# Strassen's method in the second block's first product, and a reordered first block

## The chip, the cores and the metric

The kernel runs on one core of a Trainium2 chip. The time is that of the device, in microseconds (us), from one execution to the next of the same program; the profile is that of one further execution. Engines go by their short names: PE is TensorE's matmul, PEld its weight load, DVE VectorE, ACT ScalarE, POOL GpSimd, SP SyncE, which only issues DMAs here.

## The reference

```
attn_out = decay attention of q, k, v, f        # batch 4, 8 heads, 576 tokens, head width 64
x = attn_out as 2304 tokens x 512
h = x @ w_in                                    # 512 x 2048, first block
g = where(h >= 1, h, where(h <= -1, 0, (h + 1) ** 2 / 4))
x = g @ w_out                                   # 2048 x 512
h = x @ w_in2                                   # second block, same sizes
g = (a0 + a1 h + a2 h^2 + a3 h^3) / (1 + |b0||h| + |b1|h^2 + 1e-6)
out = g @ w_out2
```

All of it is float32. The weights come as 64-bit numbers and are turned into float32 on the chip.

## The kernel before

Every product of float32 matrices is made of three fast matmuls: each operand is split into a high part (`xh`, `wh`, `gh`) and the rest (`xl`, `wl`, `gl`), and high by low, low by high and high by high are added up in PSUM. The split takes one cast on ACT and one subtraction on DVE or POOL.

The program has three stages. The first is attention over 16 pairs of heads, with some work of the first block (`filling`) laid between: the weight conversions of `w_steps`, and for two chunks of tokens the first four slices of the hidden width. The second stage is the first block, the third the second block. Both blocks go through the 2304 tokens in five chunks (`CH` = 512, 512, 512, 512, 256) and through the 2048 hidden units in 16 slices `g` of 128. For a chunk `x` and a slice `g`, `gemm_in` (L758) makes a tile h of 128 hidden units by the chunk's tokens with 4 x 3 matmuls, the activation turns it into g, `split_g_hi` and `split_g_lo` split it, and `gemm_out` adds its share to the chunk's accumulators (L852 in the first block, L854 in the second). The tiles h have four PSUM banks (tag `h`), the accumulators the other four (`a0` to `a3`), and there are three pairs of buffers for gh and gl.

The first block's activation is `a11` (clip of h to -1..1, DVE L777), `a12` (square, ACT L782) and `a21` (maximum with h, DVE L786). The second block's is a chain over ACT (`b_abs` L793, `b_sq` L796, `b_lin` L799, `b_ln` L814, `b_exp` L817), DVE (L807, L811, L821, L824, L828) and POOL (L803), and ends with `b_t4`, which frees the PSUM bank.

A planner (`plan`) sets the order of all this: each `task` has a key, an engine, an expected duration, the tasks it depends on, and the buffers it takes and frees. The planner lays the tasks out one after the other by the time at which each could start, plus a small weight times the key. The table `NUDGE` moves the keys of numbered tasks. The result is a fixed order of instructions on each engine, and an engine executes its own in that order. SP issues all DMAs, in its own fixed order.

## Time and profile before

| | |
|---|---|
| time, median of 3 runs | 971.06 us (970.61 to 971.22) |
| the profiled execution's own time | 970.89 us |
| its span, first to last instruction | 969.2 us |
| PE busy | 956.1 us, 99% of the span |
| DVE, ACT, POOL busy | 73%, 65%, 45% |
| mean granted clock of TensorE | 0.997 of full speed |

Busy time is an average over stages: attention takes the first 215 us or so, the first block runs from there to about 570 us, the second block to the end.

### The profile page before, as it was taken

What the parts mean: (1) busy time and instruction counts of PE and PEld (TensorE: products, weight loads), DVE (VectorE), ACT (ScalarE), POOL (GpSimd) and SP (SyncE); (2) the same over time, 40 slices, a digit from 0 to 9 for tenths busy, and PEclk for the clock granted to TensorE, in tenths of its full rate; (3) what the DMA queues carried; (4) which work ended last, traced back from release to release, by engine and by line L of the source; (5) the groups of instructions that cost most, each with busy time, mean ns of one, the idle gap of its engine ahead of it and who ended that gap; (6) DMA issues with size and microseconds to landing.
All of it is one profiled execution on the core that took longest, in us unless ns stands there. A gap on an engine that the chain in (4) does not pass through costs nothing.

```text
span 969.2 us, 15465 instructions
## 1 busy us (share of the span) xinstructions
PE 956.1 (99%) x5124; PEld 783.1 (81%) x5124; DVE 707.6 (73%) x1391; ACT 629.7 (65%) x1327; POOL 436.0 (45%) x490
## 2 busy tenths in 40 slices
PE   8999999999999999999999999999999999999998
PEld 5667777778888888888888998888888888888887
DVE  7898889963878967867755779776666766766565
ACT  6999888875654434334334579777677677766675
POOL 3766745636455422322221235444445454444444
PEclk9999999999999999999999999999999999999999
DMA  7897798756553565755742650010101100010010
GB/s 231 256 287 236 230 284 283 246 174 197 189 192 110 163 209 161 238 174 158 244 131 88 196 168 7 1 44 0 44 12 33 44 1 23 0 44 1 1 44 23
DMA packets 66656, 125.14 MB, mean 129 GB/s; under 512 B 10048, under 2 KB 20944, under 8 KB 66576
## 3 DMA queue, kind: packets, MB, share of 16 engines
q1 hardware_dynamic: 66576, 124.16, 40.0%
q8 instruction: 40, 0.66, 0.3%
q14 instruction: 40, 0.33, 0.1%
HBM read 94.61 MB, written 29.51 MB: 128 GB/s over the span
## 4 chain that ended last, share of the span: by engine, by line
PE 80%; DVE 2%; ACT 1%; issue 0%; POOL 0%; ACTq 0%
PE h L758 38%; PE a L854 20%; PE a L852 17%; PE T L533 1%; PE O L570 1%; PE a L839 1%; PE S L469 1%; DVE wd L113 1%; DVE wd L107 0%; DVE wd L101 0%; PE S L460 0%; ACT wh L127 0%; ACT t L782 0%; DVE t L786 0%; POOL wl L131 0%
## 5 line engine op out<-in xcount | busy, mean ns | idle before, releaser
L772 POOL TENSOR_TENSOR gl<-t,gh 128x512 fp32r<-128x512 f32 (+1 forms) x160 | 196.3, 1228 | 278.7 <-ACT gh L768 202.2
L758 PE MATMUL h<-xh,wl 128*128 128x512 f32 (+1 forms) x640 | 236.9, 370 | 0.2 <-POOL wl L131 0.2
L758 PE MATMUL h<-xl,wh 128*128 128x512 f32 (+1 forms) x640 | 235.5, 368 | 0.0
L758 PE MATMUL h<-xh,wh 128*128 128x512 f32 (+1 forms) x640 | 235.5, 368 | 0.0
L768 ACT CAST gh<-t 128x512 fp32r<-128x512 f32 (+1 forms) x160 | 93.0, 582 | 117.1 <-PE a L854 47.2
L803 POOL TENSOR_TENSOR t<-t,t 128x512 f32<-128x512 f32 (+1 forms) x80 | 94.5, 1181 | 129.5 <-ACT t L796 121.2
L758 PEld LDWEIGHTS h<-xh,wl 128*128 128x128 f32 x640 | 120.6, 188 | 20.9 <-POOL wl L131 0.6
L758 PEld LDWEIGHTS h<-xh,wh 128*128 128x128 f32 x640 | 120.6, 188 | 20.0
L758 PEld LDWEIGHTS h<-xl,wh 128*128 128x128 f32 x640 | 120.7, 189 | 19.8
L854 PE MATMUL a<-wh,gl 128*128 128x512 f32 x288 | 112.2, 389 | 0.0
L854 PE MATMUL a<-wl,gh 128*128 128x512 f32 x288 | 112.2, 389 | 0.0
L854 PE MATMUL a<-wh,gh 128*128 128x512 f32 x288 | 112.0, 389 | 0.0
L852 PE MATMUL a<-gh,wl 128*128 128x512 f32 (+1 forms) x288 | 105.3, 366 | 0.0
L852 PE MATMUL a<-gl,wh 128*128 128x512 f32 (+1 forms) x288 | 105.3, 365 | 0.0
L852 PE MATMUL a<-gh,wh 128*128 128x512 f32 (+1 forms) x288 | 105.2, 365 | 0.0
L782 ACT ACTIVATE t<-t 128x512 f32<-128x512 f32 (+1 forms) x80 | 47.1, 589 | 75.8 <-DVE t L777 75.6
L777 DVE TENSOR_SCALAR t<-h 128x512 f32<-128x512 f32 (+1 forms) x80 | 50.8, 635 | 60.2 <-PE h L758 59.7
L821 DVE SCALAR_TENSOR_TENSOR t<-t,na,h 128x512 f32<-128x512 f32 (+1 forms) x80 | 55.3, 691 | 53.3 <-ACT h L817 52.4
L521 ACT ACTIVATE P<-P,nm 128x384 f32<-128x384 f32 (+3 forms) x144 | 84.1, 586 | 15.6 <-DVE nm L509 14.6
L807 DVE TENSOR_TENSOR t<-h,t 128x512 f32<-128x512 f32 (+1 forms) x80 | 51.0, 637 | 55.4 <-ACT t L799 55.1
L238 POOL TENSOR_SCALAR_AFFINE_SELECT cb<-cb 128x128 f32<-128x128 f32 (+1 forms) x150 | 56.2, 387 | 62.9 <-DVE nm L509 47.4
L793 ACT ACTIVATE t<-h,ab 128x512 f32<-128x512 f32 (+1 forms) x80 | 51.8, 649 | 43.5 <-PE h L758 43.5
(121 smaller groups left out, 1883.6 us busy)
## 6 DMA issues: line engine op xcount, KB each, us to landing
raw<-in_moe_w_in_dram SPq DMA_DIRECT2D x32, 512.0 KB, 3.7
raw<-in_moe_w_out_dram SPq DMA_DIRECT2D x32, 512.0 KB, 4.2
xr<-xd SPq DMA_DIRECT2D x48, 256.0 KB, 3.9
wfd<-wd SPq DMA_DIRECT2D x42, 256.0 KB, 4.2
wf<-wfd SPq DMA_DIRECT2D x42, 256.0 KB, 2.6
cb<-cd SPq DMA_DIRECT2D x15, 576.0 KB, 9.4
ks<-in_k_dram SPq DMA_DIRECT2D x16, 288.0 KB, 4.7
qs<-in_q_dram SPq DMA_DIRECT2D x16, 288.0 KB, 4.7
```

The lines of the kernel that those rows point to most:

```text
L238: POOL.affine_select(out=t, in_=t, compare_op=ALU.is_ge, fill=-BIG, base=0, pattern=[[-1, n]], channel_multiplier=1,)
L521: ACT.activation(p, p, AF.Exp, scale=-1.0, bias=nm[pr][:, pos:pos + 1], accum_out=ls[pr][:, COL[pos]:COL[pos] + 1])
L758: PE.matmul(hps[g], ww[:, kk * P:(kk + 1) * P], xx[kk], start=(kk == 0 and y == 0), stop=(kk == KD - 1 and y == 2))
L768: ACT.copy(gt[g][0], mid[g][0])
L772: eng.tensor_tensor(out=lo, in0=mid.pop(g)[0], in1=hi.bitcast(F32), op=ALU.subtract)
L777: DVE.tensor_scalar(out=c, in0=hps[g], scalar1=-1.0, scalar2=1.0, op0=ALU.max, op1=ALU.min)
L793: ACT.activation(mid[g]["w"], hps[g], AF.Abs, scale=ab[:, 0:1])
L803: POOL.tensor_tensor(out=vv, in0=vv, in1=mid[g]["w"], op=ALU.add)
L807: DVE.tensor_tensor(out=t, in0=hps[g], in1=t, op=ALU.mult)
L821: DVE.scalar_tensor_tensor(out=t, in0=t, scalar=na[:, 0:1], in1=hps[g], op0=ALU.add, op1=ALU.mult)
L852: PE.matmul(acc[x, d], ww[:, dd], gg, start=st, stop=sp)
L854: PE.matmul(acc[x, d], gg[:, dd], ww[:], start=st, stop=sp)
```

## The change

In the second block, the first product is taken for six parts of 384 tokens, two at a time (three groups `s`), and for pairs of slices, g = 2j and 2j+1 (eight values of `j`). For each of the 24 steps (s, j), the pair of slices and the pair of token parts by the two halves of the 512-long sum form a product of 2 x 2 blocks. Strassen's method, in Winograd's form, makes it of seven products of blocks (`q_mul`, numbered 1, 2, 7, 6, 4, 5, 3 in the order in which they run) where eight were needed; each is 2 x 3 matmuls of 384 columns. Products 1, 6 and 5 and then 3 add up in one PSUM bank (written h<s>_<j>_0 below), 7 and 4 in a second (_1), 2 in a third (_2); a fourth (_3) takes a sum. Between them `q_copy` copies a bank to SBUF after products 1, 7 and 6 (below c1, c7 and c6; on ACT or DVE), and `q_add` on DVE adds such a copy to a bank after products 2, 4 and 5 (below a2, a1 and a3). Product 6 has to wait for c1, 4 for c7, 5 for c6, and 3 for a3, since each of them writes on in the bank that is read there. The four sums are the four tiles h of the step, and each goes through the second block's activation as before, on 384 columns.

The sums of weight blocks (`q_sums`, on DVE or POOL) are made once during the first block, split, and stored in DRAM; `q_load` brings a step's four operands back, for each group s anew, into a ring of six slots. The sums of token parts (`p_sum`) are made for each group and stored too, and `u_load`, `u_hi` and `u_lo` load and split the operands of a group. The second product (`gemm_out2`) is as before, for parts of 384 tokens: three accumulators (`a0` to `a2`), so that the fourth bank is free for the sums.

In the first block, `a11` becomes a relu on ACT, `a12` squares it, and `a21` takes max(h, 1) and the minimum of the two in one DVE instruction. The chunk of 256 tokens now comes before the last pass of a 512 chunk. In attention, the scores of query block 0 are made together with those of block 1, and pair 0's first inputs are brought in by two DMAs (`ct`) instead of four. `NUDGE` is a new table.

```diff
     def load_c(pr):
...
+        if not pr:
+            for x in range(2):
+                SP.dma_start(ct[0][x:P:QB, :].bitcast(F32), ft[0:2, 2 + x, :].bitcast(F32))
+            return
...
-            for x in range(2):
-                SP.dma_start(ct[0][j * QB + x:j * QB + x + 1, :].bitcast(F32), ft[j:j + 1, 2 + x, :].bitcast(F32))
...
-                qc = slice(b * P, (b + 1) * P)
+                parts = [(b, slice(0, (b + 1) * P))] + [(0, slice(2 * P, 3 * P))] * (b == 1)
                 for x, (qq, kk_) in enumerate(((ql_, kh), (qh, kl_), (qh, kh)) + (((one, c_),) if pr == 0 else ())):
+                    for bb_, to in parts:
+                        for jj in range(2):
+                            pp = slice(jj * QB, (jj + 1) * QB)
+                            PE.matmul(
+                                ts[jj][:, to], qq[pp, bb_ * P:(bb_ + 1) * P] if x < 3 else qq[pp, :],
+                                kk_[pp, 0:(bb_ + 1) * P], start=(x == 0 and bb_ == b),
+                                stop=(x == (2 if pr else 3)), skip_group_check=(b == 1),
+                            )
...
     def a11(g, n):
-        c = t_new(g, "t0", n, 2 if filling else TN[0])
         s = t_new(g, "t1", n, SF if filling else TN[1])
-        DVE.tensor_scalar(out=c, in0=hps[g], scalar1=-1.0, scalar2=1.0, op0=ALU.max, op1=ALU.min)
-        mid[g] = [s, c]
+        ACT.activation(s[:, 0:n], hps[g], AF.Relu, scale=0.5, bias=0.5)
+        mid[g] = [s]
 
     def a12(g):
-        s, c = mid[g]
-        ACT.activation(s, c, AF.Square, scale=0.5, bias=0.5)
+        s = mid[g][0][:, 0:hps[g].shape[1]]
+        ACT.activation(s, s, AF.Square)
 
     def a21(g):
-        s = mid[g][0]
-        DVE.tensor_tensor(out=s, in0=hps.pop(g), in1=s, op=ALU.max)
+        h = hps.pop(g)
+        s = mid[g][0][:, 0:h.shape[1]]
+        DVE.scalar_tensor_tensor(out=s, in0=h, scalar=1.0, in1=s, op0=ALU.max, op1=ALU.min)
...
+    def q_sums(j, i, e):
+        wg, wo = (wst[1, 2 * j + k, 0] for k in range(2))
+        a = [w[:, (2 * c + i) * P:(2 * c + i + 1) * P] for w in (wg, wo) for c in range(2)]
+        t = wsum[j, i] = t_new(f"q{j}", "t0", DM, TN[0])
+        s1, s2, s3, s4 = (t[:, k * P:(k + 1) * P] for k in range(4))
+        eng = ENGINES[e]
+        eng.tensor_tensor(out=s1, in0=a[2], in1=a[3], op=ALU.add)
+        eng.tensor_tensor(out=s2, in0=s1, in1=a[0], op=ALU.subtract)
+        eng.tensor_tensor(out=s3, in0=a[0], in1=a[2], op=ALU.subtract)
+        eng.tensor_tensor(out=s4, in0=a[1], in1=s2, op=ALU.subtract)
+
+    def q_hi(j, k):
+        src = wst[1, 2 * j + k, 0] if k < 2 else wsum.pop((j, k - 2))
+        hi = homes.pop(0).bitcast(F32R)
+        wq[j, k] = (hi, src)
+        ACT.copy(hi, src)
+
+    def q_lo(j, k, e):
+        hi, src = wq[j, k]
+        lo = (homes.pop(0) if k < 2 else src).bitcast(F32R)
+        wq[j, k] = (hi, lo)
+        ENGINES[e].tensor_tensor(out=lo, in0=src, in1=hi.bitcast(F32), op=ALU.subtract)
+
+    def q_store(j, k):
+        hi, lo = wq.pop((j, k))
+        c = slice(HQ * P * (k == 1), DM)
+        SP.dma_start(wqd[j, k, 0][:, c], hi[:, c].bitcast(F32))
+        SP.dma_start(wqd[j, k, 1][:, c], lo[:, c].bitcast(F32))
+        homes.extend([hi.bitcast(F32)] + [lo.bitcast(F32)] * (k < 2))
+
+    def q_load(s, j, k, c0):
+        r = ring.pop(0)
+        t = slot(r) if r >= W_EARLY else wearly.tile([P, 2, DM], F32R, tag=f"w0_{r}", name=f"q{s}_{j}_{k}")
+        wring[s, j, k] = r, t
+        SP.dma_start(t[:, :, c0:].bitcast(F32), wqd[j, k, :, :, c0:].rearrange("y p n -> p y n"))
...
+    def p_sum(s, i, y, e):
+        o, a, b = (xq[s, i, c][:, 0:QN] for c in TSUMS[y])
+        ENGINES[e].tensor_tensor(out=o, in0=a, in1=b, op=ALU.subtract)
...
+    PRODUCTS = {
+        1: (0, 0, "a", 0, True), 2: (0, HQ, "b", 2, True), 7: (None, 2, "f", 1, True), 6: (None, 1, "e", 0, False),
+        5: (None, 0, "d", 0, False), 4: (1, HQ, "g", 1, False), 3: (None, 3, "c", 0, False),
+    }
+    bank = {}
+
+    def h_new(s, j, n, spare):
+        if n == 2 and not spare:
+            t = psA.tile([P, 512], F32, tag="a3", name=f"h{s}_{j}_{n}")
+        else:
+            t = psH.tile([P, 512], F32, tag="h", name=f"h{s}_{j}_{n}")
+        bank[s, j, n] = t[:, 0:QN]
+
+    def q_mul(s, j, n, spare):
+        part, c0, y, bk, new = PRODUCTS[n]
+        if new:
+            h_new(s, j, bk, spare)
+        o = bank[s, j, bk]
+        for i in range(HQ):
+            if part is None:
+                w, c = wring[s, j, 2 + i][1], c0 * P
+            else:
+                w, c = wring[s, j, part][1], (c0 + i) * P
+            wh, wl = (w[:, z, c:c + P] for z in range(2))
+            xh, xl = xu[y, i]
+            for z, (ww, xx) in enumerate(((wl, xh), (wh, xl), (wh, xh))):
+                PE.matmul(
+                    o, ww, xx, start=(new and i == 0 and z == 0), stop=(i == HQ - 1 and z == 2), skip_group_check=True,
+                )
+        if n == 3:
+            hps[2 * j, 2 * s] = o
+        for k in {2: (0,), 4: (1,), 3: (2, 3)}.get(n, ()):
+            ring.append(wring[s, j, k][0])
+
+    def q_add(s, j, n):
+
+        to, add, v = {1: (2, 2, (2 * j, 2 * s + 1)), 7: (3, 0, (2 * j + 1, 2 * s)), 6: (1, 1, (2 * j + 1, 2 * s + 1))}[n]
+        if to == 3:
+            h_new(s, j, 3, False)
+        hps[v] = bank[s, j, to]
+        DVE.tensor_tensor(out=hps[v], in0=bank[s, j, add], in1=us.pop((s, j, n)), op=ALU.add)
+
+    def q_copy(s, j, n, e):
+        us[s, j, n] = xp.tile([P, NM], F32, tag="xr", name=f"us{s}_{j}_{n}", bufs=XR)[:, 0:QN]
+        copy(e, us[s, j, n], bank[s, j, PRODUCTS[n][3]])
+
+    def gemm_out2(x, g, d):
+        if g == 0:
+            acc[x, d] = psA.tile([P, 512], F32, tag=f"a{d}", name=f"b{x}_{d}")
+        (gh, gl), (wh, wl) = gt[g, x], wt[1, g, 1]
+        dd = slice(d * P, (d + 1) * P)
+        for y, (gg, ww) in enumerate(((gl, wh), (gh, wl), (gh, wh))):
+            PE.matmul(acc[x, d], gg[:, dd], ww, start=(g == 0 and y == 0), stop=(g == NF - 1 and y == 2))
...
-    passes = [(0, x, early) for x in range(FILL, HEAD)] + [(0, x, late) for x in range(HEAD)]
-    passes += [(0, x, range(NF)) for x in range(HEAD, NCH)]
-    passes += [(1, x, range(NF)) for x in range(NCH, 2 * NCH)]
+    passes = [(0, x, early) for x in range(FILL, HEAD)] + [(0, x, late) for x in range(HEAD - 1)]
+    passes += [(0, x, range(NF)) for x in range(HEAD, NCH)] + [(0, HEAD - 1, late)]
...
+            t = task(key, "act", ca, lambda g=g: a12(g), (t,))
+            t = task(key, "dve", cd + 0.06, lambda g=g: a21(g), (t,), (), ("h",))
...
+            prev_in = p1 = mul(1, [ql[0]], ("h",))
+            c1 = cpy(1, p1)
+            prev_in = p2 = mul(2, [], (cbank,), ("r",))
+            a2 = addu(1, (p2, c1))
+            prev_in = p7 = mul(7, [ql[2], ql[3]], ("h",))
+            c7 = cpy(7, p7)
+            prev_in = p6 = mul(6, [c1])
+            c6 = cpy(6, p6)
+            prev_in = p4 = mul(4, [c7, ql[1]], (), ("r",))
+            a1 = addu(6, (p4, c6))
+            prev_in = p5 = mul(5, [c6])
+            a3 = addu(7, (p5, c7), ("h",))
+            prev_in = p3 = mul(3, [a3], (), ("r", "r"))
+            now = []
+            for g, x, t, hb in ((2 * j, 2 * s + 1, a2, cbank), (2 * j + 1, 2 * s, a3, "h"), (2 * j, 2 * s, p3, "h"), (2 * j + 1, 2 * s + 1, a1, "h")):
+                v = (g, x)
+                ta = task(key, "act", cs + 0.09, lambda v=v: b_abs(v, QN), [t, *last_t], ("t0", "t1", "t2"))
...
+    for n, x in enumerate(2 * s + 1 - c for s in range(NSUP) for c in range(2)):
+        for g in range(NF):
+            key = K2 - LEAD + LAG + (n * NF + g) * step / 4
+            t = gsplit = task(key - KS2, "act", ca, lambda v=(g, x): split_g_hi(v, QN), (tg[g, x], gsplit), ("g",))
+            t = task(key - KS2, "pool", cp, lambda v=(g, x): split_g_lo(v, POOL), (t,), (), ("t1",))
+            for d in range(QN // P):
+                tout = last_out[d] = task(
+                    key, "pe", mm(DM, 3), lambda x=x, g=g, d=d: gemm_out2(x, g, d),
+                    [t, wd[1, g, 1], last_out.get(d), tout], (f"a{d}",) if g == 0 else (), ("g",) if d == QN // P - 1 else ()
...
-        (648, 29, -0.8), (1339, 23, 1.6), (1564, 5, 0.5), (1173, 66, -1.2), (4043, 36, 0.6), (240, 8, -16.0),
...
+        (1307, 58, 1.3), (1243, 58, 6.2), (792, 35, -3.0), (618, 16, -8.4), (1400, 59, 0.8), (884, 3, 5.1),
```

PE, in the second block of the kernel before, at chunk 7 (512 tokens) and slice 5: h7_5 is the tile (its last three matmuls), a6_0 an accumulator of the chunk before.

```order
L758 MATMUL h7_5_8901<-xh7_3_8635,wl0_1_5_6709 128x512
L758 MATMUL h7_5_8901<-xl7_3_8639,wh0_1_5_6708 128x512
L758 MATMUL h7_5_8901<-xh7_3_8635,wh0_1_5_6708 128x512
L854 MATMUL a6_0_8286<-wh1_1_14_7360,gl_8829 128x512
L854 MATMUL a6_0_8286<-wl1_1_14_7361,gh_8828 128x512
L854 MATMUL a6_0_8286<-wh1_1_14_7360,gh_8828 128x512
```

PE, in the changed kernel, at step s = 2, j = 3, from the end of product 4 to product 3 and past it: b2_0 to b2_2 are the accumulators of the second product, u and q (or arena) the operands.

```order
L1029 MATMUL h2_3_1_10429<-ul3_9754,q2_3_1_10305 128x384
L1029 MATMUL h2_3_1_10429<-uh3_9753,q2_3_1_10305 128x384
L1029 MATMUL h2_3_0_10384<-arena_3838,q2_3_2_10181 128x384 x3
L1029 MATMUL h2_3_0_10384<-arena_3838 128x384 x3
L1055 MATMUL b2_0_9984<-w1_1_12_7596,gl_10392 128x512
L1055 MATMUL b2_0_9984<-w1_1_12_7596,gh_10391 128x512 x2
L1055 MATMUL b2_1_9994<-w1_1_12_7596,gl_10392 128x512
L1055 MATMUL b2_1_9994<-w1_1_12_7596,gh_10391 128x512 x2
L1029 MATMUL h2_3_0_10384<-arena_3838,q2_3_2_10181 128x384 x3
L1029 MATMUL h2_3_0_10384<-arena_3838 128x384 x3
L1055 MATMUL b2_2_10003<-w1_1_12_7596,gl_10392 128x512
L1055 MATMUL b2_2_10003<-w1_1_12_7596,gh_10391 128x512 x2
```

The tile's twelve matmuls in a row have become products of six. Between product 5 (h2_3_0, after h2_3_1) and product 3 (h2_3_0 again), between which a3 stands, there are six matmuls of the second product; between products 4 and 5 there is nothing.

ACT, in the second block of the kernel before, at the same tile h7_5.

```order
L793 ACTIVATE t0_5_8926<-h7_5_8901,ab_68 128x512
L796 ACTIVATE t2_5_8928<-h7_5_8901,rt_69 128x512
L799 ACTIVATE t1_5_8927<-h7_5_8901,na_67 128x512
L768 CAST gh_8957<-t1_1_8750 128x512
L814 ACTIVATE t0_5_8926<-t2_5_8928 128x512
L817 ACTIVATE h7_5_8901<-t0_5_8926 128x512
L793 ACTIVATE t0_6_8969<-h7_6_8944,ab_68 128x512
```

ACT, in the changed kernel, from the end of step s = 0, j = 6 into j = 7: us0_7_7 is the copy c7, us0_7_6 the copy c6, L843 the logarithm, L846 the exponential that writes back to the bank, L793 here the cast to gh, L822, L825 and L828 the three that were L793, L796 and L799, L996 the cast of a token operand.

```order
L793 CAST gh_8295<-home_6796 128x384
L822 ACTIVATE t0_14_1_8300<-h0_7_2_8270,ab_68 128x384
L843 ACTIVATE t0_12_0_8240<-t2_12_0_8241 128x384
L825 ACTIVATE t2_14_1_8301<-h0_7_2_8270,rt_69 128x384
L397 COPY us0_7_7_8324<-h0_7_1_8303 128x384
L828 ACTIVATE t1_3840<-h0_7_2_8270,na_67 128x384
L397 COPY us0_7_6_8339<-h0_7_0_8231 128x384
L843 ACTIVATE t0_14_1_8300<-t2_14_1_8301 128x384
L846 ACTIVATE h0_6_0_8067<-t0_12_0_8240 128x384
L996 CAST arena_3838<-arena_3838 128x384
L846 ACTIVATE h0_7_2_8270<-t0_14_1_8300 128x384
```

Operations of one tile stood together; now those of two tiles of a step and of the next step are mixed, and the copies c7 and c6 of step 7 stand ahead of the exponential of step 6's tile h0_6_0, that of product 3.

## Rows read from the trace of the kernel before

**Rows 1.** The page's part 1: busy time, share of the span, instructions.
```profile
span 969.2 us, 15465 instructions
PE 956.1 (99%) x5124; PEld 783.1 (81%) x5124; DVE 707.6 (73%) x1391; ACT 629.7 (65%) x1327; POOL 436.0 (45%) x490
```

**Rows 2.** Busy time by stretch: PE, PEld, DVE, ACT, POOL; PEclk, DMA share, GB/s.
```profile
12.00:100.00 88.00, 83.05 (x637) 59.87 (x635) 78.29 (x250) 80.68 (x241) 55.05 (x98) 0.98 0.83 260
100.00:215.00 115.00, 113.32 (x881) 86.79 (x877) 99.17 (x300) 100.01 (x284) 63.06 (x113) 1.00 0.78 249
215.00:570.00 355.00, 354.79 (x1736) 300.68 (x1733) 253.28 (x400) 158.93 (x283) 124.34 (x97) 1.00 0.54 175
570.00:905.00 335.00, 335.00 (x1505) 278.43 (x1504) 235.53 (x348) 245.17 (x413) 161.53 (x126) 1.00 0.08 24
905.00:945.00 40.00, 40.00 (x228) 35.15 (x227) 20.82 (x50) 25.10 (x63) 17.35 (x21) 1.00 0.08 27
966.00:969.20 3.20, 0.00 (x0) 0.00 (x0) 0.22 (x1) 0.00 (x0) 0.00 (x0) 0.73 0.44 164
```

**Rows 3.** Chain that ended last: start, length, what, matmuls in it.
```profile
588.65 2.72 PE a L854 x12
591.37 2.72 PE h L758 x12
...
901.45 4.31 PE h L758 x36
```

**Rows 4.** Timeline of PE in attention: pairs of 384-column matmuls on half arrays.
```profile
123.17 0.35 PE L469 MATMUL S<-kl,qh 64*128 64x384 f32 x2
123.34 0.35 PE L469 MATMUL S<-kh,qh 64*128 64x384 f32 x2
```

**Rows 5.** Groups by shape, PE, whole span: count; busy, mean ns; idle before.
```profile
L758 PE MATMUL h<-xh,wl 128*128 128x512 f32 x512 | 200.7, 392 | 0.2 <-POOL wl L131 0.2
...
L758 PE MATMUL h<-xh,wl 128*128 128x256 f32 x128 | 36.1, 282 | 0.0
```

**Rows 6.** Timeline in the second block: a tile's last matmul, ACT, then DVE.
```profile
653.54 0.39 PE L758 MATMUL h<-xh,wh 128*128 128x512 f32 x1
...
653.97 0.69 ACT L793 ACTIVATE t<-h,ab 128x512 f32<-128x512 f32 x1 [0.31 <-PE h L758]
...
655.12 0.78 ACT L799 ACTIVATE t<-h,na 128x512 f32<-128x512 f32 x1
...
655.94 0.69 DVE L807 TENSOR_TENSOR t<-h,t 128x512 f32<-128x512 f32 x1 [0.17 <-ACT t L799]
```

**Rows 7.** Groups by shape, DVE and ACT, 570 to 960 us.
```profile
L807 DVE TENSOR_TENSOR t<-h,t 128x512 f32<-128x512 f32 x64 | 44.2, 691 | 41.4 <-ACT t L799 41.2
L807 DVE TENSOR_TENSOR t<-h,t 128x256 f32<-128x256 f32 x16 | 6.8, 422 | 14.0 <-ACT t L799 13.9
L793 ACT ACTIVATE t<-h,ab 128x512 f32<-128x512 f32 x64 | 44.3, 693 | 43.5 <-PE h L758 43.5
L793 ACT ACTIVATE t<-h,ab 128x256 f32<-128x256 f32 x16 | 7.5, 475 | 0.0
L381 ACT COPY osb<-a 128x512 f32<-128x512 f32 x8 | 4.7, 592 | 1.2 <-PE a L854 1.2
L381 ACT COPY t<-a 128x256 f32<-128x256 f32 x4 | 1.4, 388 | 0.0
```

**Rows 8.** Groups by shape, DVE and ACT, 20 to 215 us.
```profile
L777 DVE TENSOR_SCALAR t<-h 128x512 f32<-128x512 f32 x8 | 5.5, 689 | 1.7 <-PE h L758 1.6
...
L782 ACT ACTIVATE t<-t 128x512 f32<-128x512 f32 x8 | 5.1, 633 | 3.7 <-DVE t L777 3.7
```

**Rows 9.** PE's waits, whole span: total us, times, longest.
```profile
PE S L460 <- DMA ct<-ft: 1.0, 1, 1.0
```

**Rows 10.** Timeline of SP at the start: the four DMAs of ct.
```profile
7.00 2.48 SPq L233 DMA_DIRECT2D ct<-ft  x4
```

**Rows 11.** The page's part 6: DMA issues, KB each, median us to landing.
```profile
raw<-in_moe_w_in_dram SPq DMA_DIRECT2D x32, 512.0 KB, 3.7
```

More of the change, by code (lines that the diff above doesn't have):

```diff
@@ L123, in s0 @@
         def s0():
-            pool = wearly if g < W_EARLY else wpool["late"]
             at["s"] = wst.pop((m, g, half))
-            at["w"] = [pool.tile([P, DM], F32R, tag=f"{x}{half}_{g}", name=f"w{x}{half}_{m}_{g}") for x in "hl"]
-            ACT.copy(at["w"][0][:], at["s"])
+            if half == 0 and g >= W_EARLY:
+                t = slot(g)
+            else:
+                pool = wearly if g < W_EARLY else wpool["late"]
+                t = pool.tile([P, 2, DM], F32R, tag=f"w{half}_{g}", name=f"w{half}_{m}_{g}")
+            at["w"] = [t[:, 0, :], t[:, 1, :]]
+            ACT.copy(at["w"][0], at["s"])
         def s1(eng=POOL):
             hi, lo = at["w"]
-            eng.tensor_tensor(out=lo[:], in0=at["s"], in1=hi[:].bitcast(F32), op=ALU.subtract)
+            eng.tensor_tensor(out=lo, in0=at["s"], in1=hi.bitcast(F32), op=ALU.subtract)
             wt[m, g, half] = (hi, lo)
@@ L749 @@
     hps, gt, mid, acc, po = {}, {}, {}, {}, {}
+    given = {}
     def gemm_in(m, x, g, kks):
@@ L761, in gemm_in @@
                 )
+        if kks[-1] == KD - 1 and not filling:
+            ring.extend(given.get((x, g), ()))
+    homes = []
     def t_new(g, tag, n, bufs):
+        if tag == "t1" and not filling:
+            return homes.pop(0)
         return tp.tile([P, NM], F32, tag=tag, name=f"{tag}_{g}", bufs=bufs)[:, 0:n]
@@ L1036, with more_small @@
     last_out = {}
-    prev_in = None
+    prev_in = gsplit = None
+    a11s, ins = [], {}
+    PREP = ((4, 10), (4, 15)), ((3, 7), (3, 10)), ()
+    LA = (XSLOT - W_EARLY) * 2 * DM
+    GIVES = {g: ([g] if g < XSLOT else [], []) for g in range(NF)}
+    for g in range(XSLOT):
+        GIVES[g][1].append("r")
+    for n, (y, i) in enumerate(UNITS):
+        GIVES[W_EARLY + (LA + (n + 1) * 2 * QN - 1) // (2 * DM)][1].append(f"u{y}{i}")
+    NSM = 4 * DM // QN
+    def more_small():
+        t = wpool["late"].tile([P, 4 * DM], F32, tag="tail", name="tailh")
+        homes.extend(t[:, k * QN:(k + 1) * QN] for k in range(NSM))
     for p, (m, x, fs) in enumerate(passes):
@@ L1085 @@
-            t = task(key, "act", ca, lambda g=g, n=n: split_g_hi(g, n), (t,), ("g",))
-            t = task(key, "pool", cp, lambda g=g: split_g_lo(g, POOL), (t,), (), ("t1",))
-            for d in range(nd):
+                deps = [prev_in, wd[0, g, 0]] + [sx[kk] for kk in kks if one]
+                prev_in = task(key, "pe", mm(n, 3 * len(kks)), lambda x=x, g=g, kks=kks: gemm_in(0, x, g, kks), deps,
+                               ("h",) if kks[0] == 0 else (),
+                               (tuple(f"x{kk}" for kk in kks) if end else ()) + (tuple(gone) if kks[-1] == KD - 1 else ()))
@@ new lines @@
+            t = tin = ins[x, g] = prev_in
+            lastg = ends and end
+            t = task(
+                key, "act", cs + 0.09, lambda g=g, n=n, lastg=lastg: (a11(g, n), lastg and more_small()), (t, *a11s[-1:], *(qstored.values() if lastg else ())),
+                ("t1",), ("t1",) * NSM if lastg else ()
+            )
+            a11s.append(t)
+            t = task(key, "act", ca, lambda g=g: a12(g), (t,))
+            t = task(key, "dve", cd + 0.06, lambda g=g: a21(g), (t,), (), ("h",))
@@ new lines @@
+            ko = key + (KOL if ends else KO[0]) * step
+            t = gsplit = task(ko - KO[0] if ends else key, "act", ca, lambda g=g, n=n: split_g_hi(g, n), (t, gsplit), ("g",))
+            t = task(ko - KO[0] if ends else key, "pool", cp, lambda g=g: split_g_lo(g, POOL), (t,), (), ("t1",))
+            if add and g == fs[-2 if ends else -4]:
+                for d in range(KD):
+                    loads[d] = task(
+                        ko if ends else key, "sp", ld(n), lambda x=x, d=d: part_load(x, d), [lastpass[x, d], tout if ends else tin, *prev_evac], ("t2",)
+                    )
@@ L1109 @@
-            if m == 0 and uses[0, g][0] == p:
-                for half in range(2):
-                    k = base + min(sizes[p, g] + 1.5 * half + 0.5, needs[1, g] + KO[1] * half - W2L)
-                    tag = ("d", "raw")[half]
-                    u = (1, g, half)
-                    t = task(k, "sp", ld(DM), lambda u=u: w_load(*u), tuple(stored.values()), (tag,))
-                    split(u, k, 0.0, t, tag, W2E, ((tin, tout)[half],))
-        if m == 0:
-            prev_evac = outs
+                ek = ko + KEV
```

359 lines of the change are left out of this document (257 added, 102 removed), and 14 rows, old and new, of the table NUDGE.

## The prediction

> **What bounds the kernel now.** I read the page's busy shares first: PE stands at 99% of 969.2 us, and the next, DVE, at 73% [rows 1]. A share of busy time is not yet a bound, so I went to the stretches [rows 2]. From 215 to 945 us PE has no idle time that counts (354.79 of 355, then 335 of 335, then 40 of 40), at the full granted clock (1.00, the 2.4 GHz level), while ACT and DVE have a quarter or more of their time to spare. That PE is not only busy but at its pace shows in the chain of work that ended last [rows 3]: from there on it is all matmuls, and twelve of 512 columns take 2.72 us, whichever product they belong to, 36 of 256 columns 4.31 us. So a matmul costs 226.7 ns at 512 columns and 119.7 ns at 256; the 392 and 282 ns in the groups [rows 5] are the durations of pipelined instructions, which overlap. In attention the engines are closer: PE 83 of 88 us, ACT 80.7, DVE 78.3 up to 100 us, then PE 113.3 of 115 [rows 2]. The last 3 us hold no matmul: a copy and a store [rows 2].
>
> So what the change takes from PE in the second block comes off the end, as long as no wait for ACT, DVE or a DMA takes its place.
>
> **The product itself.** The first product of the second block is now 16 slices of 4 x 3 matmuls for each of five chunks: 768 of 512 columns and 192 of 256 (half of the counts of both blocks, 3 x 512 and 3 x 128 [rows 5]). That is 768 x 0.2267 + 192 x 0.1197 = 197.1 us. Afterwards it is 24 steps of seven products of six matmuls, 1008 of 384 columns. No full-height matmul of 384 columns is in the trace. Half way between the two prices lies 173.2 ns; two side by side on half arrays take 0.17 us from start to start [rows 4]; without any fixed part it would be 0.75 x 226.7 = 170 ns. I take 173.2 ns: 174.6 us, **22.5 us less**, with 25.7 us as the other end. The second product keeps its matmuls (864 of 512 columns), and the first block and attention theirs.
>
> A step is then 42 x 0.1732 + 36 x 0.2267 = 15.4 us of PE.
>
> **Can the other engines follow?** Their work per tile is that of today, on 384 columns. ACT is busy for 245.2 of 335 us among tiles of 512 columns (5.44 us of PE each, so 4.0 us of ACT) and for 25.1 of 40 among tiles of 256 (12 x 0.1197 + 6 x 0.2267 = 2.8 us of PE, so 1.8 us) [rows 2]. Half way, 2.9 us, four tiles: 11.5 us a step. The three copies are between 388 and 592 ns each on ACT [rows 7], half way 0.49, so 1.5 us if ACT makes all: 13.0 of 15.4 us, 84%. For DVE the same sum gives 3.8 and 1.5, half way 2.6, so 10.6 us, and three adds, between 422 and 691 ns, 1.7 us: 12.3 us, 80%. POOL stays at half. PE remains the longest, by 2.4 us a step. The loads of split weights, 3.5 times 512 KB a step (24 steps, 44 MB), are 119 GB/s over a stretch where 24 GB/s flow now and where 260 have flowed in attention [rows 2]; a DMA of 512 KB lands after 3.7 us [rows 11], and a slot is given back about a step, 15 us, before its next content is needed. That is covered.
>
> **The new waits.** The danger is not load but delay. A result reaches ACT about 0.04 us after the matmul's modelled end (653.54 + 0.39, then 653.97), and an engine hands on to DVE in as much (655.12 + 0.78, then 655.94) [rows 6]; that end lies some 0.16 us past the matmul's 227 ns slot. So c7, c6 take 0.16 + 0.04 + 0.49 + 0.04 = 0.73 us on ACT and 0.80 on DVE, if nothing is ahead of them, and a3 0.80. In the changed order, product 4 follows product 7 with only product 6 between in 18 of 24 steps, and product 5 follows 6 with only product 4 between in 19: 1.04 us of PE work, so 0.24 to 0.31 us to spare. Between 5 and 3 stand six matmuls of the second product (1.36 us, 0.56 to spare), in three steps three (0.68, short by 0.12). c1 has 2.08 us or more. Behind a late copy stands the whole PE queue, since PE runs in order. An operation of ACT or DVE on 384 columns is about 0.55 us (half way between the durations of rows 7), so a copy that arrives in the middle of one loses 0.28 us on average and just passes, and one that has a whole operation ahead loses 0.25 to 0.3 us of PE. I could not tell for 48 copies which it is. Nothing (all pass) is one end; 48 x 0.27 = 13 us (all are behind one) the other. I take 0.1 us each, **+5 us**, nearer to nothing since the engines have a sixth or more of their time free and the chance of a free or half-done engine is the greater.
>
> Then the banks. Product 7 of the next step needs one of the four. The tile whose exponential runs earliest of the three that hold one gives it back: in step (2, 4), from the ACT order, 13 operations (0.485 us from start to start, the 0.575 of rows 6 scaled by the ratio of L793's half way 0.584 to 0.693 [rows 7]) and four of DVE after, 8.3 us behind product 5; product 7 stands 9.2 us of PE work behind it. No wait.
>
> **The first block.** a11 leaves DVE for ACT. At 512 columns DVE takes 689 ns from PSUM [rows 8], and ACT's operation from PSUM, L793, 693 ns [rows 7]: an even exchange. The Trainium skill's page "ScalarE: Activation LUTs", section "Rules for kernel authors", says to give relu, max and min to VectorE and not to ScalarE, which is up to about 3 times slower in bf16. In float32 from PSUM the rows do not show that factor; by it the eight relus of attention would be some 17 us of ACT's time (an estimate from the page's factor and L777's 689 ns), and the sum below, if ACT led there, some 969 us. From 215 to 570 us ACT is busy for 158.9 of 355 us [rows 2]; 56 relus of 0.69 and 16 of 0.475 [rows 7] add 46 us, and 16 more casts of split weights at the 0.63 of L782 [rows 8] 10 us, so 215 of 355: covered by PE's own 355. DVE loses as much, and gets at most 64 additions and 16 splits of weights and 24 sums of tokens (0.42, 0.69 and 0.56 each at the most [rows 7], 51 us): it stays near 253 of 355. Cost: nothing; without that cover it would be some 56 us. In attention it is eight relus, 5.5 us on an engine that is busy for 100 of 115 us [rows 2]. PE leads there, and DVE becomes freer by as much: I take nothing, with 5.5 us as the upper end and the same gain (DVE feeds PE's transposes and scores too) held to be at most 1 us.
>
> **The start.** PE waits 1.00 us for `ct` [rows 9], whose four DMAs take 2.48 us to issue [rows 10]. Two take half. I take -1.0 us, between -1.6 (1.24, and the casts of pair 0 pulled forward) and nothing (the wait goes over to another input).
>
> The tail stays: last copy, last store.
>
> **Sum.** The profiled execution is 970.9 us, 1.7 more than its span and 0.2 less than the median. 970.9 - 22.5 - 1.0 + 5 = **952.4, so 952 us**, faster by 2%. What a measurement of this kernel can tell from no change is about 0.2%, that is 1.9 us.
>
> **The rivals.**
> *Late copies.* The copies and adds come behind other operations in most steps. For it: 84% and 80% of load, and only 0.3 us to spare. Against it: rows 2 show no PE wait today where ACT is at 73%. 970.9 - 22.5 - 1 + 13 = 960 us.
> *Banks in strict turn.* If product 7 of a step had to wait for the last of the four tiles, that of product 3, its price would be: 18 ACT operations and five of DVE from the moment that a1 is ready, 8.6 us after product 3's end. In the changed order PE has 5.5 to 10.9 us of work in between (6.84 in five steps, 5.48 in two, 6.16 in two); what is short adds up to 23 us over the steps. 970.9 - 22.5 - 1 + 5 + 23 = 976 us, **slower**. It turns from gain to loss at about 18.5 us, 0.8 us a step. Against it: in the order shown, the copy c7 of step 7 stands ahead of the exponential of step 6's product 3 tile, on the same engine, so product 7 had its bank before that.
> *ACT bounds attention.* The eight relus come through at full price: 958 us. Against it: PE at 113.3 of 115 us.
> *384 columns cost what 512 do.* The change would not save but add: 1008 x 0.2267 = 228.5 against 197.1, some 1006 us. Against it: 256 columns cost 0.53 of 512, and rows 4.
>
> **How the numbers follow.** Forecast, 947 to 957 us (waits of 0 to 10): 0.66. Late copies, 957 to 964: 0.16. ACT in attention, around 958: 0.06. A gain beyond the forecast, waits near nothing and a price of 170 ns, down to 944: 0.05. Banks or another wait that eats all, 969 to 980: 0.06, half of it above 973 and half within 1.9 us of no change. 384 columns at full price: 0.01. The range is 944 to 964. Faster 0.93, same 0.03, slower 0.04.
>
> **What would show it.** In the changed trace: matmuls of 384 columns 173 ns apart; the second block shorter by some 18 us from its first activation to the end; PE idle in it some 5 us in all, ended by ACT or DVE at products 4, 5 and 3 and not by a DMA; ACT near 84% there; the `ct` wait gone. I am wrong if PE waits at product 7 in each step, if attention ends later than now, or if the first block shows idle PE: ACT, DVE or the weight sums would then not be hidden.

## The result, and the profile after

The changed kernel takes 956.8 us, median of four runs (955.9 to 958.4), the kernel before 971.0 (970.6 to 971.2). The ratio is 0.9856, 95% interval 0.9839 to 0.9873. That is 14.2 us less where 18.5 were forecast, inside the range, and 0.2 us inside the forecast's own band of 947 to 957 us: the number alone does not tell it from the rival of late copies (957 to 964). The profiled execution is the slowest of the four, 958.4 us with a span of 956.7.

The page's part 1 of the changed kernel, against [rows 1]:
```profile
span 956.7 us, 16614 instructions
PE 938.7 (98%) x5172; PEld 791.6 (83%) x5172; DVE 758.6 (79%) x1614; ACT 706.1 (74%) x1568; POOL 462.3 (48%) x542
```
Its stretches, with the columns of [rows 2]:
```profile
12.00:100.00 88.00, 81.47 (x643) 59.28 (x640) 79.97 (x262) 78.66 (x238) 53.34 (x99) 0.96 0.82 260
100.00:215.00 115.00, 113.17 (x864) 87.25 (x863) 100.80 (x301) 99.15 (x274) 60.92 (x110) 1.00 0.78 248
215.00:570.00 355.00, 351.76 (x1740) 299.21 (x1739) 262.30 (x445) 211.26 (x396) 127.58 (x101) 1.00 0.64 217
570.00:905.00 335.00, 333.78 (x1670) 300.30 (x1669) 292.40 (x565) 289.62 (x613) 194.02 (x189) 1.00 0.50 168
905.00:945.00 40.00, 40.00 (x185) 33.89 (x184) 14.16 (x27) 19.22 (x39) 20.16 (x20) 1.00 0.06 21
```
From 570 to 905 us DVE went from 70 to 87% and ACT from 73 to 86%. PE still leads, but where it had 0.2 us of idle time from 215 to 905 us it now has 4.5.

Three pieces of the chain that ended last (columns as in [rows 3]):
```profile
220.44 10.91 PE h L777 x48
...
871.49 6.26 PE h L1029 x36
...
911.27 41.54 PE b L1055 x183
```
The second piece prices the new product: 36 matmuls of 384 columns in 6.26 us, 173.9 ns each. The first is the start of the main stage, at 220.44 us; the chain before has the same piece at 220.94 us. From there to the end of the span there are 736.3 us, against 748.3 before: 12.0 us, where the product alone should have saved 21.8 (197.1 - 1008 x 0.1739). Some 10 us were given back on the way. PE's waits from 215 us on (total us, times, longest) say where to look:
```profile
PE h L1029 <- DVE h L1043: 1.5, 1, 1.5
PE h L1029 <- DVE t L857: 0.8, 1, 0.8
PE h L1029 <- ACT gh L793: 0.6, 1, 0.6
PE h L777 <- DVE t L814: 0.5, 1, 0.5
PE a L879 <- DVE t L890: 0.5, 1, 0.5
PE b L1055 <- DVE osb L399: 0.5, 1, 0.5
```
There is no row for a DMA, and each wait occurs once: nothing recurs in 24 steps. The sum, 4.4 us, is less than 10, since the modelled end of a matmul lies past its 174 or 227 ns slot and so hides part of each gap. Counted from start to start of the matmuls, against slots of 226.7, 173.9 and 119.7 ns, the gaps from 221 us on add up to 9.9 us, where the kernel before has 0.6: 6.7 us in 19 gaps of over 40 ns (5.9 of them at these six waits), and 3.0 us in 365 gaps of 5 to 30 ns. The two largest gaps stand in the first step of the second block. This is the timeline there (start, us, engine, line, what):
```profile
552.20 0.54 DVE L1000 TENSOR_TENSOR arena<-arena 128x384 fp32r<-128x384 f32 x1
...
553.39 1.16 POOL L832 TENSOR_TENSOR t<-t,t 128x384 f32<-128x384 f32 x1 [2.47 <-ACT t L825]
...
553.75 1.69 DVE L1000 TENSOR_TENSOR arena<-arena 128x384 fp32r<-128x384 f32 x2
...
555.36 0.54 DVE L399 COPY us<-h 128x384 f32<-128x384 f32 x1
...
556.05 1.29 PE L1029 MATMUL h<-arena,q 128*128 128x384 f32 x6 [0.63 <-ACT gh L793]
556.18 1.29 POOL L798 TENSOR_TENSOR gl<-t,gh 128x512 fp32r<-128x512 f32 x1 [1.62 <-ACT gh L793]
556.48 2.69 DVE L1000 TENSOR_TENSOR arena<-arena 128x384 fp32r<-128x384 f32 x2
...
557.74 1.02 POOL L832 TENSOR_TENSOR t<-t,t 128x384 f32<-128x384 f32 x1 [0.27 <-ACT t L825]
...
559.57 0.55 DVE L1043 TENSOR_TENSOR h<-h,us 128x384 f32<-128x384 f32 x1
...
560.26 0.94 PE L1029 MATMUL h<-arena,q 128*128 128x384 f32 x4 [1.53 <-DVE h L1043]
```
L1000 is the subtraction that leaves the low part of a token operand. Both its inputs lie in SBUF, and alone it takes 0.54 to 0.55 us (the one at 552.20). The pair at 556.48 took 2.69: POOL was in its own two-input operations from 556.18 to 557.47 and from 557.74 to 558.76, and the pair ended at 559.17, 0.41 us behind the second. Behind it in DVE's queue stands a3, the addition that product 3 waits for. Before product 5 the copy c6 (555.36) stands in the same way behind the pair at 553.75, with POOL at work from 553.39 to 554.55. "ACT gh" in the row of 556.05 is only the last event seen; that cast feeds another product.

From this came the theory, "boundaries" in the first expectations and "entry" once the hand-over between token groups had shown only the single waits of 0.8 and 0.5 us above: the largest new waits come from DVE being late while token operands are prepared, its subtractions held up by POOL, with copies and additions queued behind. The first rival was "late copies": copies come late in the steady steps, as the forecast's +5 had it.

### The profile page after: what moved, and what is told of

The parts are those of the page before. It is cut to its first block, busy times and chain, and to the rows that moved or that the text cites. A ratio compares the mean times of both kernels' runs of the same rounds, so it can differ in the third digit from the quotient of the medians.

```text
span 956.7 us, 16614 instructions
## 1 busy us (share of the span) xinstructions
PE 938.7 (98%) x5172; PEld 791.6 (83%) x5172; DVE 758.6 (79%) x1614; ACT 706.1 (74%) x1568; POOL 462.3 (48%) x542
## 4 chain that ended last, share of the span: by engine, by line
PE 81%; DVE 9%; DMA 5%; ACT 2%; issue 2%; SPq 0%; DVEq 0%; ACTq 0%
PE b L1055 20%; PE h L1029 17%; PE h L777 17%; PE a L879 15%; PE T L551 3%; PE O L588 3%; PE S L485 2%; PE a L868 2%; DMA cb<-cd 1%; DVE P L527 1%; DMA wqd<-t 1%; DVE wd L109 1%; DVE arena L1000 1%; PE S L476 1%; DMA qs<-in_q_dram 1%
## 5 line engine op out<-in xcount | busy, mean ns | idle before, releaser
L798 POOL TENSOR_TENSOR gl<-t,gh 128x512 fp32r<-128x512 f32 (+2 forms) x125 | 146.7, 1179 | 213.5 <-ACT gh L793 176.3
L1055 PE MATMUL b<-w,gh 128*128 128x512 f32 x576 | 179.1, 392 | 0.0
L879 PE MATMUL a<-gh,w 128*128 128x512 f32 (+1 forms) x576 | 161.8, 366 | 0.0
L832 POOL TENSOR_TENSOR t<-t,t 128x384 f32<-128x384 f32 x96 | 99.3, 1037 | 94.9 <-ACT t L825 93.4
L1055 PEld LDWEIGHTS b<-w,gh 128*128 128x128 f32 x576 | 108.0, 188 | 21.1
L777 PE MATMUL h<-xh,arena 128*128 128x512 f32 (+1 forms) x400 | 120.0, 368 | 0.5 <-DVE t L814 0.5
L879 PEld LDWEIGHTS a<-gh,w 128*128 128x128 f32 x576 | 104.0, 189 | 17.1
L1055 PE MATMUL b<-w,gl 128*128 128x512 f32 x288 | 112.1, 389 | 0.5 <-DVE osb L399 0.5
L793 ACT CAST gh<-t 128x512 fp32r<-128x512 f32 (+2 forms) x125 | 68.8, 553 | 50.9 <-PE a L879 17.9
L879 PE MATMUL a<-gl,w 128*128 128x512 f32 (+1 forms) x288 | 105.4, 366 | 0.6 <-DVE t L890 0.5
L1029 PE MATMUL h<-arena,q 128*128 128x384 f32 x459 | 93.5, 337 | 2.9 <-DVE h L1043 1.5
L822 ACT ACTIVATE t<-h,ab 128x384 f32<-128x384 f32 x96 | 56.1, 584 | 13.6 <-DVE h L1043 12.8
```

Source lines behind the costliest of these rows:

```text
L777: PE.matmul(hps[g], ww[:, kk * P:(kk + 1) * P], xx[kk], start=(kk == 0 and y == 0), stop=(kk == KD - 1 and y == 2))
L793: ACT.copy(gt[g][0], mid[g][0][:, 0:n])
L798: eng.tensor_tensor(out=lo, in0=t[:, 0:lo.shape[1]], in1=hi.bitcast(F32), op=ALU.subtract)
L822: ACT.activation(mid[g]["w"], hps[g], AF.Abs, scale=ab[:, 0:1])
L832: POOL.tensor_tensor(out=vv, in0=vv, in1=mid[g]["w"], op=ALU.add)
L879: PE.matmul(acc[x, d], ww[:, dd], gg, start=(first and y == 0), stop=(last and y == 2))
```

## The experiments

Differences are from the changed kernel's 956.8 us unless another is named; the kernel before took 971.4 to 971.7 us beside these runs, and the ratios are to that.

**No copies.**
```
 def q_copy(s, j, n, e):
-    us[s, j, n] = xp.tile(...)
-    copy(e, us[s, j, n], bank[s, j, PRODUCTS[n][3]])
+    pass
...
 def q_add(s, j, n):
-    DVE.tensor_tensor(out=hps[v], in0=bank[s, j, add], in1=us.pop((s, j, n)), op=ALU.add)
+    DVE.tensor_copy(hps[v], bank[s, j, add])
```


> The 72 copies of partial products out of PSUM (48 of them ahead of the next product on the same bank) are left out, and the 72 additions become copies from bank to bank; order and everything else as in the changed kernel (956.8 us). Theory 'boundaries' (the some 10 us of new PE idle stem from DVE running late where token operands are prepared, at the entry of the second block and at the hand-over between token groups): 954 to 956 us, since the additions and the late DVE remain. Rival 'late copies' (the idle comes from copies that reach ACT or DVE too late in the steady steps): 947 to 949 us, nearly all of the 10 us back.

**No residuals of tokens.**
```
 def u_lo(y, i, e):
...
-    ENGINES[e].tensor_tensor(out=lo, in0=lo.bitcast(F32), in1=hi.bitcast(F32), op=ALU.subtract)
+    pass
```


> The 42 subtractions that make the low part of the token operands of the second block (L1000) are left out, so PE's products no longer wait for them and DVE and POOL lose 42 operations; everything else as in the changed kernel (956.8 us). Theory 'boundaries': these operations stand on DVE for 1.2 to 1.7 us instead of 0.54 when POOL works beside them, and additions behind them come late; without them 951 to 954 us, and the gaps before products at 540 to 600 us shrink from 3.9 us to under 1.5. Rival 'late copies': 956 to 957 us, no change.

They took 953.5 us (ratio 0.9811, 0.9798 to 0.9824) and 953.7 us (0.9815, 0.9801 to 0.9828). Without all 72 copies 3.3 us came back, not 10: late copies in every step are refuted. (The additions stay in this run, as copies; among the waits above, the row of L1043, the additions, is a single one, that of the first step.) Without the 42 subtractions 3.1 us came back, and it is the same 3 us. The stretch of the entry, in which PE was busy for 57.84 of 60 us in the changed kernel, without copies (columns of [rows 2]):
```profile
540.00:600.00 60.00, 60.00 (x300) 53.69 (x300) 50.87 (x95) 49.21 (x101) 35.62 (x31) 1.00 0.66 214
```
The same stretch without residuals:
```profile
540.00:600.00 60.00, 60.00 (x299) 53.44 (x298) 44.92 (x87) 51.73 (x107) 35.48 (x31) 1.00 0.64 211
```
The waits of the entry need both, subtractions that are held up and copies in the same queue; taking either away ends them. Without the copies DVE reaches the pair ahead of a3 at 554.58 us, 0.49 us before POOL's next operation begins, and the pair takes 1.01 us. That the additions alone would keep part of it, as the expectation had it, was wrong.

**No product 5.**
```
 def q_mul(s, j, n, spare):
...
+    if n == 5:
+        return
```


> The 144 matmuls of product 5 are left out, one product of seven in each step. If PE sets the pace of the steps and a matmul of 384 columns costs 173.2 ns, 24.9 us go: 932 us (931 to 933). If ACT or DVE are close to setting the pace (by the forecast's sum ACT has 13.0 of 15.4 us a step, 13.0 of 14.4 without this product), the gain is smaller and waits for ACT or DVE appear in the steady steps: 936 to 940 us.

It took 950.0 us (0.9774, 0.9756 to 0.9792; its four runs 947.4 to 951.8): of 24.9 us of PE work only 6.8 came off the end, less than either expectation had. PE's longest wait from 540 us on in that run:
```profile
PE h L1031 <- DVE h L1045: 12.1, 17, 3.4
```
A place in its timeline where it arises:
```profile
702.46 0.56 DVE L1045 TENSOR_TENSOR h<-h,us 128x384 f32<-128x384 f32 x1
...
702.92 0.55 DVE L836 TENSOR_TENSOR t<-h,t 128x384 f32<-128x384 f32 x1
...
703.39 0.56 DVE L1045 TENSOR_TENSOR h<-h,us 128x384 f32<-128x384 f32 x1
...
704.00 1.31 PE L1031 MATMUL h<-arena,q 128*128 128x384 f32 x6 [0.94 <-DVE h L1045]
```
Product 3 (704.00) now waits for a3 (703.39), which stands on DVE behind a1 (702.46) and an operation of the activation. DVE is not out of time (177.5 of 205 us busy from 700 to 905 us): it is a matter of turn. Taken away at this place, PE work comes off the end by some 0.3 us a step (6.8 us over 24 steps), not by the 1.04 us of the product or the 2.4 us by which PE leads in load. But product 5 also stood between a1 and a3 and covered DVE's work there: without it, 1.36 us of the second product are left in most steps to cover both additions, which by the forecast's own prices take 0.16 + 0.04 + 2 x 0.55 + 0.04 = 1.34 us with nothing between them (an estimate). So the run measures this place; whether work taken elsewhere in the step would come through better, no run shows.

**Loads.**
```
 def q_load(s, j, k, c0):
     r = ring.pop(0)
+    if s:
+        wring[s, j, k] = r, kept[r]
+        return
...
```


> The loads of the split weights for the second and third token group (two thirds of the 96 ring loads) are left out; the products then use what the ring holds from the first group. Everything else as in the changed kernel (956.8 us). Forecast: the loads are covered, 956 to 957 us. Rival 'loads slow the steps' (a slot comes free too late, or the transfers slow others): 953 us or less, and waits before products at 600 to 900 us disappear.

It took 956.1 us (0.9844, 0.9826 to 0.9861): no change, as forecast, though from 570 to 905 us the traffic fell from 168 to 79 GB/s. The loads are covered.

**The clip back on DVE.**
```
 def a11(g, n):
...
-    ACT.activation(s[:, 0:n], hps[g], AF.Relu, scale=0.5, bias=0.5)
+    DVE.tensor_scalar(out=s[:, 0:n], in0=hps[g], scalar1=-1.0, scalar2=1.0, op0=ALU.max, op1=ALU.min)
 def a12(g):
...
-    ACT.activation(s, s, AF.Square)
+    ACT.activation(s, s, AF.Square, scale=0.5, bias=0.5)
 def a21(g):
...
-    DVE.scalar_tensor_tensor(out=s, in0=h, scalar=1.0, in1=s, op0=ALU.max, op1=ALU.min)
+    DVE.tensor_tensor(out=s, in0=h, in1=s, op=ALU.max)
```


> The first block's activation as in the kernel before (clip on DVE, square with scale and bias on ACT, maximum on DVE), at the places in the order of the changed kernel; the order of the other engines is the same, and the result too. The forecast put the exchange at nothing: 956 to 958 us. Rival 'relu on ACT holds up attention': 952 to 955 us. Rival 'DVE has no room for it' (where DVE's delays end PE's waits already): 959 to 962 us, with more PE idle between 100 and 570 us.

It took 967.7 us (0.9955, 0.9942 to 0.9967), 10.9 more and beyond all three expectations: taking back the exchange that the forecast put at nothing undoes most of the gain of 14.2 us. Its waits from 100 to 570 us, on DVE's second operation and on its sums of partial results:
```profile
PE a L879 <- DVE t L890: 3.7, 3, 1.3
PE h L777 <- DVE t L814: 2.8, 2, 1.9
```
What else DVE has to do there now is in the groups of the changed kernel from 215 to 570 us (count, busy and mean, idle before):
```profile
L936 DVE TENSOR_TENSOR t_q<-t_q,t 128x512 fp32r<-128x512 f32 x16 | 11.3, 718 | 1.3 <-ACT t L930 1.3
L936 DVE TENSOR_TENSOR t<-wd,t 128x512 fp32r<-128x512 f32 x16 | 10.5, 685 | 1.2 <-ACT t L804 1.0
...
L921 DVE TENSOR_TENSOR t_q<-wd 128x128 f32<-128x128 f32 x16 | 5.6, 350 | 0.3
L922 DVE TENSOR_TENSOR t_q<-t_q,wd 128x128 f32<-128x128 f32 x16 | 4.7, 292 | 0.5
L924 DVE TENSOR_TENSOR t_q<-wd,t_q 128x128 f32<-128x128 f32 x16 | 4.5, 284 | 0.0
L923 DVE TENSOR_TENSOR t_q<-wd 128x128 f32<-128x128 f32 x16 | 4.5, 283 | 0.0
```
That is 41 us for the weights of the second block. Two runs ask whether it is this.

**The new activation in the kernel before.**
```
 def a11(g, n):
...
-    DVE.tensor_scalar(out=c, in0=hps[g], scalar1=-1.0, scalar2=1.0, op0=ALU.max, op1=ALU.min)
+    ACT.activation(c, hps[g], AF.Relu, scale=0.5, bias=0.5)
 def a12(g):
...
-    ACT.activation(s, c, AF.Square, scale=0.5, bias=0.5)
+    ACT.activation(s, c, AF.Square)
 def a21(g):
...
-    DVE.tensor_tensor(out=s, in0=hps.pop(g), in1=s, op=ALU.max)
+    DVE.scalar_tensor_tensor(out=s, in0=hps.pop(g), scalar=1.0, in1=s, op0=ALU.max, op1=ALU.min)
```


> The kernel before, with the activation of the changed kernel alone (relu with scale and bias and then square on ACT, min and max in one operation on DVE), in the order of the kernel before. The previous run showed that moving the relu back to DVE costs the changed kernel 11 us. Theory 'DVE is short only because of the new work' (weight sums, splits): the kernel before has DVE to spare in its first block, so nothing is won, 970 to 972 us. Rival 'the exchange itself wins': 960 to 966 us, and then a large part of the measured gain is not the product's.

**The clip on DVE, with little weight work.** The activation is that of the run with the clip; `dvp` stands for work that could go to DVE or POOL and was given to DVE.
```
 def q_sums(j, i, e):
...
+    if e == "dvp":
+        DVE.tensor_tensor(out=t, in0=wg, in1=wo, op=ALU.add)
+        return
 def q_lo(j, k, e):
...
+    if e == "dvp":
+        return
```


> The run with the clip on DVE (967.7 us), with most of DVE's new weight work in the first block left out (each four 128-column additions become one of 512 columns, and the 32 subtractions for the low parts are left out, some 30 us of DVE). Theory 'DVE is short because of the weight work': most of the 11 us come back, 957 to 961 us. Rival 'order' (the clip at this place of DVE's queue is late whatever else DVE does): 965 to 968 us.

In the kernel before the activation alone gives 970.0 against 971.4 us (0.9987, 0.9978 to 0.9996), 1.4 us. With the weight work gone the run with the clip takes 961.9 us (0.9897, 0.9881 to 0.9913): 5.8 of the 10.9 us are back, fewer than expected, and the two waits fall from 3.7 and 2.8 us to 1.7 and 0.5. So the move of the relu is worth little by itself; it makes room on DVE for work that the product brings. That explains half.

Some of the other half lies in attention. These are the starts of the main stage: kernel before, the same with the relu on ACT, changed kernel with the clip on DVE, changed kernel with the relu (the run below with one copy moved):
```profile
220.94 10.91 PE h L758 x48
219.35 10.90 PE h L758 x48
221.57 10.91 PE h L777 x48
219.07 10.90 PE h L777 x48
```
The granted clock from 12 to 100 us was 0.98, 1.00, 0.98 and 1.00. At 0.98 the changed kernel's runs with the relu start at 219.7 to 220.8 us, and both with the clip at 221.5 to 221.6, whatever the weight work; in the kernel before at 1.00 (the run without its table, below) it is 221.23. So in attention the relu on ACT brings some 1 to 2 us in either kernel, read from single executions. Another 1.7 us or so (an estimate) of the 10.9 is clock, in the profiled execution: in the run with the clip it stood at the 1.2 GHz level for 3.4 us from 533.7 us on, behind the wait of 1.9 us. The rest may be the clip's place in DVE's queue, chosen for ACT; no run separates that.

**All residuals on POOL**, then **those of product 3 alone**, then **one copy on ACT**.
```
 def u_lo(y, i, e):
...
-    ENGINES[e].tensor_tensor(out=lo, ...)
+    POOL.tensor_tensor(out=lo, ...)
```


> The low parts of the second block's token operands (L1000, 42 operations, 33 of them on DVE) are all made on POOL, at the same places in the order; the result is the same. Theory 'entry' (the 3 us of PE idle between 555 and 561 us come from copies and additions of DVE standing behind residuals that wait for POOL): 953 to 955 us, if POOL makes them in time; against it speaks that POOL takes longer for one. Rival 'POOL becomes late': 958 to 962 us, with PE waits for POOL at 540 to 600 us.


```
 def u_lo(y, i, e):
...
-    ENGINES[e].tensor_tensor(out=lo, ...)
+    eng = POOL if y == "c" and len(wring) < 12 else ENGINES[e]
+    eng.tensor_tensor(out=lo, ...)
```


> Of the residuals of the first token group only the last two, those of product 3's operand, go to POOL, so that DVE's addition ahead of product 3 no longer stands behind them; the result is the same. Theory 'entry': the 1.9 us of PE idle before product 3 at 558 us go, 954.5 to 955.5 us. Rival 'POOL becomes late' as in the run with all of them on POOL: the sum of squares and the residuals of the first block that stand behind on POOL come 1 us later, a bank is given back later, and PE waits at 560 to 570 us: 957 to 959 us.


```
 def q_copy(s, j, n, e):
-    copy(e, us[s, j, n], bank[s, j, PRODUCTS[n][3]])
+    copy("act" if s == 0 and j == 0 and n == 6 else e, us[s, j, n], bank[s, j, PRODUCTS[n][3]])
```


> One copy, that of product 6 in the first step, goes from DVE to ACT, where it stands between the two casts for product 3's operand; the result is the same. Theory 'entry': DVE reaches the residuals of product 3 about 0.5 us earlier, ahead of POOL's next operation at 556.2 us, and the waits of 1.0 and 1.9 us before products 5 and 3 shrink by 1 to 2 us together: 954.5 to 956 us. Rival: the cast of ACT comes 0.5 us later by as much, no change, 956.5 to 957.5 us.

The first took 964.3 us (0.992, 0.9903 to 0.9938), 7.5 more, beyond its rival's 958 to 962: POOL needs 1.0 us for one where DVE needs 0.55, and PE waits for POOL and, behind POOL's late sums, for banks. The second took 954.9 (0.9831, 0.9815 to 0.9847), as expected, and the third **953.7 us (0.9817, 0.9802 to 0.9833)**: one copy moved brings 3.1 us, more than expected, and beats both kernels. The same place in its timeline, where the copy is on ACT:
```profile
553.06 0.49 ACT L397 COPY us<-h 128x384 f32<-128x384 f32 x1
...
553.61 1.31 PE L1029 MATMUL h<-arena,q 128*128 128x384 f32 x6
...
554.06 1.02 DVE L1000 TENSOR_TENSOR arena<-arena 128x384 fp32r<-128x384 f32 x2
...
554.62 1.62 POOL L798 TENSOR_TENSOR gl<-t,gh 128x512 fp32r<-128x512 f32 x1 [2.00 <-issue]
...
555.47 0.56 DVE L1043 TENSOR_TENSOR h<-h,us 128x384 f32<-128x384 f32 x1
...
556.15 1.24 PE L1029 MATMUL h<-arena,q 128*128 128x384 f32 x6
```
DVE reaches the pair (554.06) 0.56 us ahead of POOL's operation, and the pair takes 1.02 instead of 2.69 us; now POOL's is the longer one (1.62 against 1.29). The addition comes 1.4 us after the pair's start instead of 3.1. Product 3 (556.15) no longer waits, and product 5 (553.61) some 0.3 us.

**The order without its table**, in the changed kernel and in the one before.
```
-        (2777, 10, 9.9), ... (3425, 3, 0.1),
```


> The entries of the order table that act on the stage after attention are left out, so that the planner's own order stands there; the result is the same. If the gain hangs on the product alone, 957 to 960 us. If the steps have as little room as the run without product 5 showed, additions and copies come late in many steps: 962 to 972 us, much of the gain lost, with PE idle ended by DVE in the second block.


```
-        (1564, 5, 0.5), (1922, 19, -2.9), (1996, 45, -8.4), (1547, 29, -0.9), (4043, 36, 0.6),
```


> The kernel before without the entries of its order table that act on the stage after attention (5 entries; in the changed kernel the 28 such entries were worth 27 us); the result is the same. Theory 'the new steps have little room': the steps of the kernel before leave ACT and DVE a quarter of their time and one product waits for one activation only, so the planner's own order will do there, 970 to 975 us. Rival 'any order of this length needs its table': 980 us or more.

The changed kernel took 983.8 us (1.0133, 1.0111 to 1.0154): 27 us more, beyond what was expected, and slower than the kernel before. The kernel before lost nothing (971.3 us, 0.9998, 0.9989 to 1.0008). In the changed kernel without its table, from 570 to 905 us PE was busy for 317.1 of 335 us, and its two longest waits after 540 us are for a bank (L851 here is the operation that gives one back) and for a late operand of the second product:
```profile
PE h L1023 <- DVE t L851: 7.3, 3, 3.9
PE b L1049 <- POOL gl L792: 7.2, 5, 2.8
```

## Why the prediction was right, and where its steps were not

**The product**: right. 173.9 ns a matmul against 173.2, 21.8 us against 22.5. The end at which 384 columns cost as much as 512 is out.

**The new waits, +5**: the term that was mis-sized, and its place was wrong. They are some 10 us, and the 48 copies of the steady steps are not in them. About 3 us lie in the first step. The forecast had a copy arrive in time "if nothing is ahead of them", with operations of about 0.55 us ahead. It left out that a DVE operation with two SBUF inputs takes over a microsecond when POOL is at work (1.65 us at 549.70). The other named waits are single ones, here from start to start: a bank given back late (1.0), an output copy (0.7), and two in the first block (0.7 and 0.8). Then come 0.8 us in smaller single gaps, and 3.0 in the 365 gaps of 5 to 30 ns, 2.5 of it in the second block. Without copies, without residuals and without reloads these last stay at 3.0 us, so they are none of the three; their cause stays open.

**"PE remains the longest, by 2.4 us a step"**: right as a load (86% for ACT against 84 forecast, 87% for DVE against 80), wrong as a margin. Taking out product 5, 1.04 us a step, brought only 0.3.

**Banks**: right in this order, one wait in 24 steps. Without the table PE waits 10 us for banks in six places, and the change has the other sign. That is the rival's kind of wait, though not one in every step; whether it was for the tile that the rival named is not shown.

**The first block, 0**: the loads came out (ACT 211 of 355 us against 215 forecast, DVE 262 against 253), and the relu takes 0.60 us on ACT at 512 columns, less than the 0.69 forecast. But the forecast costed only the move to ACT and not the place that it frees: with the new work on DVE the clip there costs 10.9 us. Its own sign of being wrong, idle PE in the first block, did show: from 215 to 570 us PE was idle for 3.2 us where it had been for 0.2. Of that 2.2 us are the entry of the second block, and the two waits of 0.5 us before it end with DVE.

**Attention and start, -1.0**: too small, and its reason holds only in part. The `ct` wait is gone, and the main stage begins 0.5 us earlier in the profiled execution, whose granted clock was 0.96 from 12 to 100 us, against 0.98 in [rows 2]; at 1.00 it begins at 218.8 to 219.2 in four runs, 2.0 to 2.4 us before the 221.23 of the kernel before at that clock. But the relu alone, without the new start, brings the kernel before to 219.35. That leaves 0.2 to 0.6 us for the two DMAs and the other changes in attention together, no run parts them, and the relu, put at nothing there and at most 1 us, brought some 1 to 2.

**Loads**: covered, at 168 GB/s in that stretch.

With the one copy moved the sum nearly closes, 953.7 us measured and 952.4 forecast, in part by luck: its profile still shows 7.0 us of gaps where 5 were forecast, and a main stage that starts 1.9 us earlier than that of the kernel before, where 1.0 was forecast.
